# ALiBi and the sliding window as one product with a factor per head, in place of tables on TensorE and biased exponentials on ScalarE

## The chip, the cores and the metric

The kernel runs on one core of a Trainium2 chip. The metric is the device time of one execution in microseconds (us), and every kernel is compared with the kernel before, run in the same rounds on the same chip. The kernel before took 338.57 us (median of 3 runs, 338.24 to 338.61).

## The reference

Sliding-window attention with ALiBi, followed by a feed-forward block (FFN) with a swish. Eight batches, eight heads, 576 positions, 64 numbers a head.

```python
# attention, per batch and head
scores = scale * q @ k.T
rel = pos[:, None] - pos[None, :]
bias = -slopes[h] * abs(rel)                 # slopes 2**-1 ... 2**-8
scores = where((rel >= 0) & (rel < 128), scores + bias, -1e9)
attn = softmax(scores)
x = attn @ v                                 # then 4608 tokens x 512
# FFN
h = x @ w_in                                 # 512 -> 2048
out = (h * sigmoid(beta * h)) @ w_out        # 2048 -> 512
```

The scores are small, so no maximum is subtracted. The weights of a query can be any common multiple, because the sum of the weights divides them.

## The kernel before

One core does all eight batches. TensorE is meant to be busy without a break: the FFN of earlier tokens fills what the attention of the next batch leaves. Batches 0 and 1 come in early, when little else can be done, and are transposed on TensorE in pairs of heads; batches 2 to 7 are transposed by transfers, and their attention is spread between the FFN's matmuls. A "visit" is the scores of two heads for some blocks of keys: 2 x 512 columns (visit B and all visits of batches 2 to 7) or 2 x 384 (visit A).

ALiBi and the window came about in two ways. In batch 0, in the A visits of batch 1 and in both "tail" visits (`SCT`, the last 64 queries of batches 0 and 1), a table with the bias is added on TensorE ahead of the scores, and one exponential follows. In the other visits the bias of the key is the bias pointer of the exponential, so that a visit needs four exponentials, and a product with a mask of zeros and ones follows on VectorE.

```python
def SP_(b, vis, p):                          # a visit of batch 0 or 1
    ...
    for e in range(2):                       # not in the B visits of batch 1
        nc.tensor.matmul(sps[:, e, 0:w], lhsT=ident[:], rhs=table..., start=True, stop=False)
    ...                                      # the scores, added to the table
    nc.scalar.activation(out=pt[:, :, 0:w], in_=sps[:, :, 0:w], func=ACTF.Exp, scale=qscale)

def decayed(pt, sps, p, own, w):
    for e in range(2):
        h = 2 * p + e
        for half, cols in ((0, slice(0, own)), (1, slice(own, w))):
            nc.scalar.activation(out=pt[:, e, cols], in_=sps[e][:, cols], func=ACTF.Exp,
                                 scale=qscale, bias=bias[:, half, h : h + 1])

def SC(b, m, p):                             # a visit of batches 2 to 7
    ...                                      # six matmuls: scores into SS (two banks)
    decayed(pt, sps, p, OWN[m], 512)
    nc.vector.tensor_tensor(out=pt[:], in0=pt[:], in1=masks[m][:], op=ALU.mult)

def TP(b, p):                                # transposes of a pair of heads, k (i=1) then q (i=0)
    for i in (1, 0):
        tps = psum_t.tile([P, FULL], F32, name="tps", tag="t")     # psum_t has 2 slots
        ...                                  # four matmuls with the identity
        (nc.vector.tensor_copy if b or i else nc.scalar.copy)(out=QK[...], in_=tps[:])

def betas():                                 # another user of the same two slots
    bps = psum_t.tile([P, NFF], F32, name="bps", tag="t")
    nc.tensor.transpose(out=bps[:], in_=bflat[:], identity=identf[:])
    nc.vector.tensor_scalar_mul(beta_h[:], bps[:], 0.5)

def Hm(g, j, cs):                            # FFN: four matmuls into a bank hps, then
    ...
    nc.scalar.activation(out=sig[:], in_=hps, func=ACTF.Tanh, scale=beta_h[:, j : j + 1])
    nc.vector.scalar_tensor_tensor(          # gT; it frees the bank
        out=gts[g][:, j, :], in0=sig[:], scalar=1.0, in1=hps, op0=ALU.add, op1=ALU.mult)

# start of the program (cut)
TP(0, 0); SP_(0, "A", 0); SP_(0, "B", 0); tables(2, 4); ones(); cast_pair(0, 1)
TP(0, 1); SP_(0, "A", 1); SP_(0, "B", 1); tables(4, 6); ...; PVP(0, "A", 0); betas(); cast_pair(0, 2)
TP(0, 2); tables(6, 8); ...; SP_(0, "A", 2); SP_(0, "B", 2)
TP(0, 3); PVP(0, "A", 1); SP_(0, "A", 3); SP_(0, "B", 3); ...
```

`PVP` takes weights times values and normalizes on VectorE, `XP` transposes the result for the FFN. The orders of TensorE and of GpSimd (which casts the inputs to bf16) are those of the program throughout. In the start of the program, those of VectorE and ScalarE follow from it too, as compiled.

The softmax here doesn't subtract the row's maximum and nothing guards it: scores larger than these inputs give would overflow.

## Time and profile before

| | before |
|---|---|
| median of 3 runs | 338.57 us |
| span of the profiled execution | 336.8 us |
| busy TensorE / VectorE / ScalarE / GpSimd | 320.8 / 200.0 / 207.0 / 103.5 us |
| mean granted TensorE clock | 1.00 |
| waits of the FFN's banks (hps) for gT | 4.1 us in 8 waits |

The page's busy line and the main groups are in the prediction. This is the view of busy time by stretches of the kernel before; columns: stretch, length, busy us (and instructions) of TensorE's matmuls, its weight loads, VectorE, ScalarE, GpSimd, then granted clock, share of the transfer engines, GB/s.

```profile
8.00:12.00 4.00, 3.50 (x35) 2.17 (x34) 3.70 (x12) 3.30 (x5) 3.64 (x5) 1.00 0.96 289
12.00:16.00 4.00, 3.54 (x35) 2.18 (x33) 2.88 (x7) 2.84 (x5) 3.94 (x7) 1.00 1.22 207
```

TensorE was busy 3.5 us of every 4, at the full clock. This is the start itself, in TensorE's timeline (start, us, engine, line, operation, count, and in brackets the idle time ahead of it with what ended it):

```profile
9.85 0.34 PE L299 MATMUL SS<-qkT 64*128 64x256 bf16 x4 [0.50 <-DVE qkT L252]
...
13.42 0.34 PE L299 MATMUL SS<-qkT 64*128 64x256 bf16 x4 [0.35 <-ACT qkT L252]
...
20.96 0.61 PE L502 MATMUL SX<-XT,W 128*128 128x512 bf16 x2
```

These are the scores of the second and third pair of heads and the first matmul of the FFN.

### The profile page before, as it was taken

Reading aid. Unit: us, or ns where it says so; the run is one execution under the profiler, and the core shown is the slowest. Engines: PE = TensorE matmul, PEld = TensorE weight load, DVE = VectorE, ACT = ScalarE, POOL = GpSimd, SP = SyncE. Lnnn points to the kernel's source line nnn. Section 1 sums busy time; section 2 is a strip of 40 time slices with the busy share of each in tenths; the row PEclk is TensorE's granted clock in tenths of the full one; section 3 lists DMA queues with packets and bytes.
Section 4 is the critical chain, followed back from the end, with each engine's and each line's share of the span. In section 5 each row is a group of like instructions: output and inputs, shape, how many; then the busy total and the mean of one; then the engine's idle time right before and its main releaser. Section 6 shows DMA issues by size and latency. Waiting matters only on the chain.

```text
span 336.8 us, 6208 instructions
## 1 busy us (share of the span) xinstructions
PE 320.8 (95%) x2293; PEld 155.4 (46%) x2293; DVE 200.0 (59%) x435; ACT 207.0 (61%) x405; POOL 103.5 (31%) x177
## 2 busy tenths in 40 slices
PE   8889899999998999999999999999999999999995
PEld 4545454444443454444444444444444444444444
DVE  6757897655468883766187717671778167525500
ACT  3767857565538875778469747774878465345511
POOL 4945630428345337321305142322100100010010
PEclk9999999999999999999999999999999999999999
DMA  7999999999999999991939986997120211210022
GB/s 201 241 283 224 168 201 216 202 197 256 215 224 250 176 217 253 219 201 35 219 80 193 186 200 145 214 161 173 45 58 15 78 47 49 55 64 31 0 85 73
DMA packets 146159, 51.81 MB, mean 154 GB/s; under 512 B 135360, under 2 KB 143824, under 8 KB 146128
## 3 DMA queue, kind: packets, MB, share of 16 engines
q1 hardware_dynamic: 139152, 38.29, 61.4%
q0 software_dynamic: 6944, 13.11, 16.4%
q8 instruction: 18, 0.29, 0.4%
q14 instruction: 13, 0.11, 0.1%
q10 hardware_dynamic: 32, 0.01, 0.0%
HBM read 36.71 MB, written 9.44 MB: 137 GB/s over the span
## 4 chain that ended last, share of the span: by engine, by line
PE 73%; DVE 13%; ACT 10%; issue 3%; DVEq 0%; ACTq 0%
PE ops L528 34%; PE hps L502 26%; ACT pt L319 7%; DVE gT L510 4%; PE SS L418 3%; DVE pt L426 3%; ACT sig L509 2%; PE pv L455 2%; PE hpo L502 2%; DVE qkT L252 1%; PE pv L451 1%; PE SS L103 1%; DVE xnp L337 1%; DVE xn L337 1%; PE SS L299 1%
## 5 line engine op out<-in xcount | busy, mean ns | idle before, releaser
L502 PE MATMUL hps<-XT,W 128*128 128x512 bf16 x540 | 135.2, 379 | 4.5 <-DVE gT L510 4.1
L528 PE MATMUL ops<-W,gT 128*128 128x512 bf16 (+1 forms) x592 | 138.5, 374 | 0.5 <-ACT osb L538 0.5
L510 DVE SCALAR_TENSOR_TENSOR gT<-sig,hps 128x512 bf16<-128x512 bf16 x135 | 91.2, 682 | 65.9 <-ACT sig L509 65.2
L509 ACT ACTIVATE sig<-hps,beta_h 128x512 bf16<-128x512 f32 x135 | 92.5, 695 | 56.3 <-PE hps L502 51.6
L319 ACT ACTIVATE pt<-SS,bias 128x256 bf16<-128x256 f32 (+1 forms) x192 | 75.0, 478 | 15.4 <-PE SS L418 15.4
L528 PEld LDWEIGHTS <-gT 128*128 128x128 bf16 x592 | 54.0, 98 | 57.7 <-issue 2.4
L502 PEld LDWEIGHTS <-W 128*128 128x128 bf16 x576 | 51.7, 98 | 60.5 <-issue 9.5
L545 POOL DMA_DIRECT2D out_dram<-osb x34 | 18.4, 542 | 114.0 <-ACT osb L538 113.8
L426 DVE TENSOR_TENSOR pt<-pt,mask 128x1024 bf16<-128x1024 bf16 x48 | 35.6, 742 | 26.6 <-ACT pt L319 26.5
L538 ACT ACTIVATE osb<-ops 128x512 f32<-128x512 f32 (+1 forms) x28 | 16.6, 592 | 38.3 <-PE ops L528 38.3
L226 POOL CAST vs<-fst 128x512 bf16<-128x512 f32 (+1 forms) x40 | 26.0, 657 | 34.3 <-DMA fst<-in_v_dram 31.2
L211 POOL CAST bst<-fst 128x512 bf16<-128x512 f32 (+1 forms) x32 | 20.7, 646 | 49.0 <-DMA fst<-in_q_dram 35.0
L337 DVE TENSOR_TENSOR xn<-pv,zs 128x256 bf16<-128x256 f32 (+1 forms) x62 | 25.9, 421 | 1.6
L212 POOL CAST bst<-fst 128x512 bf16<-128x512 f32 (+1 forms) x32 | 20.6, 644 | 18.1 <-DMA fst<-in_k_dram 17.9
L455 PE MATMUL pv<-vs,pt 128*128 128x65 bf16 x240 | 21.4, 193 | 0.0
L455 PEld LDWEIGHTS <-pt 128*128 128x128 bf16 x240 | 16.5, 97 | 8.4
L418 PE MATMUL SS<-qkT 64*128 64x256 bf16 (+2 forms) x240 | 18.9, 252 | 1.0 <-ACT pt L319 0.8
L418 PEld LDWEIGHTS <-qkT 64*128 64x128 bf16 x240 | 8.2, 94 | 21.2 <-issue 20.7
L451 PE MATMUL pv<-vs,pt 128*128 128x65 bf16 x192 | 17.9, 193 | 0.0
L451 PEld LDWEIGHTS <-pt 128*128 128x128 bf16 x192 | 15.2, 98 | 5.5
L536 DVE TENSOR_SCALAR osb<-ops 128x512 f32<-128x512 f32 (+1 forms) x9 | 5.9, 657 | 18.6 <-PE ops L528 18.5
L336 DVE RECIPROCAL zs<-pv 128x4 f32<-128x4 f32 (+1 forms) x66 | 11.3, 173 | 9.3 <-PE pv L455 8.2
(83 smaller groups left out, 176.5 us busy)
## 6 DMA issues: line engine op xcount, KB each, us to landing
out_dram<-osb POOLq DMA_DIRECT2D x34, 256.0 KB, 3.1
fst<-in_k_dram SPq DMA_DIRECT2D x32, 256.0 KB, 5.1
fst<-in_q_dram SPq DMA_DIRECT2D x32, 256.0 KB, 4.8
fst<-in_v_dram SPq DMA_DIRECT2D x32, 256.0 KB, 4.4
W<-in_moe_w_in_dram POOLq DMA_DIRECT2D x4, 512.0 KB, 7.3
W<-in_moe_w_out_dram POOLq DMA_DIRECT2D x4, 512.0 KB, 10.7
fst<-in_q_dram SPq DMA_DIRECT2D x8, 128.0 KB, 4.1
fst<-in_k_dram SPq DMA_DIRECT2D x8, 128.0 KB, 4.0
```

Source lines behind the costliest of these rows:

```text
L211: nc.gpsimd.tensor_copy(out=t[0:rows, 0], in_=fs.pop(("q", b, sb))[0:rows])
L226: return nc.gpsimd.tensor_copy(out=VS[b % 2][0:rows, sb, :, 0:D], in_=fs.pop(("v", b, sb))[0:rows])
L319: nc.scalar.activation(out=pt[:, e, cols], in_=sps[e][:, cols], func=ACTF.Exp, scale=qscale, bias=bias[:, half, h : h + 1],)
L337: nc.vector.tensor_tensor(out=xn, in0=pv[0:nq, :, 0:D], in1=zs[0:nq].broadcast_to([nq, 4, D]), op=ALU.mult)
L418: nc.tensor.matmul(o, lhsT=qk[64 * e : 64 * e + 64, 1, p, P * kb : P * kb + P], rhs=qk[64 * e : 64 * e + 64, 0, p, P * kb : P * kb + nq], ...
L426: nc.vector.tensor_tensor(out=pt[:], in0=pt[:], in1=masks[m][:], op=ALU.mult)
L451: nc.tensor.matmul(pv[:, hl, 0 : D + 1], lhsT=weights(b, qb - 1, h, 1), rhs=vs[:, qb - 1, h, 0 : D + 1], start=True, stop=False,)
L455: nc.tensor.matmul(pv[:, hl, 0 : D + 1], lhsT=weights(b, qb, h, 0), rhs=vs[:, qb, h, 0 : D + 1], start=qb == 0, stop=True,)
L502: nc.tensor.matmul(hps, lhsT=W1[:, c, bass.ts(j, P)], rhs=XT[:, c, c0 : c0 + TOKG], start=(c == 0), stop=(c == NDM - 1),)
L509: nc.scalar.activation(out=sig[:], in_=hps, func=ACTF.Tanh, scale=beta_h[:, j : j + 1])
L510: nc.vector.scalar_tensor_tensor(out=gts[g][:, j, :], in0=sig[:], scalar=1.0, in1=hps, op0=ALU.add, op1=ALU.mult)
L528: nc.tensor.matmul(ops_[:, cols], lhsT=gT[:, j, i * P : i * P + P], rhs=W2[:, j, cols], start=(j == 0), stop=(j == NFF - 1),)
```

## The change

The intent: scores are plain in every visit, one exponential covers the whole visit, and ALiBi and the window together are one factor, exp(−slope · distance) inside the window and 0 outside, which takes the mask's place in the product. The tables and their matmuls go. The factors (`fall`, eight heads x 512 columns) are made by ScalarE at the start; two rearranged copies of them (`fallt` for the tails, `fall[1]` for the other kind of visit) are made by VectorE. Since batch 0 and the A visits of batch 1 get a product they did not have, the cast of q in batch 1 goes from VectorE to ScalarE.

```diff
+    def falls(h0, h1):
+        for h in range(h0, h1):
+            nc.scalar.activation(out=fall[0][:, h]..., in_=rel..., func=ACTF.Exp, scale=-slopes[h])
+    def falls_tail():                        # 2 copies of 512 columns on VectorE
+    def falls_late(i):                       # 4 copies, 512 to 1536 columns
-    def biases(): ...   def tables(h0, h1): ...   def constants_masks(): ...   def tail_masks(): ...
@@ TP
-            (nc.vector.tensor_copy if b or i else nc.scalar.copy)(
+            (nc.vector.tensor_copy if i else nc.scalar.copy)(
@@ SP_
-        ... two matmuls of a table with the identity ...
-        if not plain: ... one exponential; return
-        decayed(...)
-        nc.vector.tensor_tensor(... in1=masks[0][:, :, 0:w], op=ALU.mult)
+        nc.scalar.activation(out=pt[:, :, 0:w], in_=sps[:, :, 0:w], func=ACTF.Exp, scale=qscale)
+        nc.vector.tensor_tensor(... in1=fall[0][:, 2 * p : 2 * p + 2, 0:w], op=ALU.mult)
@@ SCT
-        ... two matmuls of a table ...
+        nc.vector.tensor_tensor(out=PC[:, 0:1024], in0=PC[:, 0:1024], in1=fallt..., op=ALU.mult)
@@ SC
-        decayed(pt, sps, p, OWN[m], 512)
-        nc.vector.tensor_tensor(out=pt[:], in0=pt[:], in1=masks[m][:], op=ALU.mult)
+        nc.scalar.activation(out=pt[:], in_=SS[:], func=ACTF.Exp, scale=qscale)
+        nc.vector.tensor_tensor(out=pt[:], in0=pt[:], in1=fall[m][:, 2 * p : 2 * p + 2], op=ALU.mult)
@@ start of the program
-            tables(2, 4) ... tables(4, 6) ... tables(6, 8)
+            falls(5, 6) ... falls(6, 7) ... falls(7, 8)      # falls(0, 5) with the constants
```

More of the change, by code (lines that the diff above doesn't have):

```diff
@@ L48 @@
     qscale = 1.0 / sqrt(D)
-    REF = 63.5
     FAR = 1.0e5
@@ L60 @@
     pen = const.tile([P, P], F32, name="pen")
-    rel = const.tile([P, 3, P], F32, name="rel")
+    rel = const.tile([P, 2, P], F32, name="rel")
     zeros = const.tile([P, 512], BF16, name="zeros")
-    table = const.tile([P, H, 3, P], BF16, name="table")
-    masks = [const.tile([P, 2, 512], BF16, name=f"mask{m}") for m in range(2)]
-    kpos = const.tile([P, 1], F32, name="kpos")
-    bias = const.tile([P, 2, H], F32, name="bias")
+    fall = [const.tile([P, H, 512], BF16, name=f"fall{m}") for m in range(2)]
+    fallt = const.tile([P, 2, 512], BF16, name="fallt")
     PC = const.tile([P, 1024 + 64], BF16, name="pc")
@@ L118, in constants @@
         make_identity(nc, identf[:])
-        nc.gpsimd.iota(
-            kpos[:], pattern=[[0, 1]], base=0, channel_multiplier=1,
-            allow_small_or_imprecise_dtypes=True,
-        )
         for a, cmp in ((0, ALU.is_lt), (1, ALU.is_ge)):
@@ L126, in constants @@
             nc.vector.scalar_tensor_tensor(
-                out=rel[:, 2 * a], in0=qtok[:], scalar=float(P * a), in1=pen[:], op0=ALU.add,
+                out=rel[:, a], in0=qtok[:], scalar=float(P * a), in1=pen[:], op0=ALU.add,
                 op1=ALU.add)
-        nc.vector.tensor_copy(out=rel[:, 1], in_=rel[:, 0])
-        tables(0, 2)
-    def tables(h0, h1):
+        falls(0, 5)
+    def falls(h0, h1):
+        t = rel[:]
         for h in range(h0, h1):
-            nc.vector.tensor_scalar_mul(table[:, h], rel[:], -slopes[h] / qscale)
+            nc.scalar.activation(
+                out=fall[0][:, h].rearrange("k (a n q) -> k a n q", a=2, n=2),
+                in_=bass.AP(tensor=t.tensor, offset=t.offset,
+                            ap=[list(t.ap[0]), [P, 2], [0, 2], [1, P]]),
+                func=ACTF.Exp, scale=-slopes[h])
+    def falls_tail():
+        for at, c in ((0, 0), (256, 256)):
+            nc.vector.tensor_copy(
+                out=fallt[:, :, at : at + 256].rearrange("k e (p q) -> k p e q", q=64),
+                in_=fall[0][:, :, c : c + 64].rearrange("k (p e) q -> k p e q", e=2))
+    def falls_late(i):
+        to, at, w = ((0, 0, 192), (192, 0, P), (320, 256, 64), (384, 256, P))[i]
+        nc.vector.tensor_copy(out=fall[1][:, :, to : to + w], in_=fall[0][:, :, at : at + w])
     def ones():
@@ L144, in padding @@
         nc.gpsimd.memset(PC[:, 1024:], 0.0)
-    def biases():
-        for h in range(H):
-            for half in range(2):
-                nc.vector.tensor_scalar(
-                    out=bias[:, half, h : h + 1], in0=kpos[:], scalar1=-(REF + half * P),
-                    scalar2=slopes[h], op0=ALU.add, op1=ALU.mult,
-                )
     def betas():
@@ L156, in betas @@
         nc.vector.tensor_scalar_mul(beta_h[:], bps[:], 0.5)
-    def fill(m, at, n, w, cmp):
-        t = qtok[:]
-        o = masks[m][:, :, at : at + n * w].rearrange("p e (n w) -> p e n w", w=w)
-        nc.vector.tensor_scalar(
-            out=o, in0=bass.AP(tensor=t.tensor, offset=t.offset,
-                               ap=[list(t.ap[0]), [0, 2], [0, n], [1, w]]),
-            scalar1=0.0, scalar2=None, op0=cmp)
-    def constants_masks():
-        fill(0, 0, 2, P, ALU.is_ge)
-        fill(0, 256, 2, P, ALU.is_lt)
-    def tail_masks():
-        fill(1, 0, 1, P, ALU.is_ge)
-        fill(1, 128, 1, 64, ALU.is_ge)
-        fill(1, 192, 1, P, ALU.is_ge)
-        fill(1, 320, 1, 64, ALU.is_lt)
-        fill(1, 384, 1, P, ALU.is_lt)
     fs = {}
@@ L270 @@
              "B": ((1, 256, 256, P), (2, 0, 256, 256), (3, 128, 384, P))}
-    PLAIN = ((1, "B"),)
     WIDTH = {"A": 384, "B": 512}
@@ L277, in SP_ @@
         w = WIDTH[vis]
-        plain = (b, vis) in PLAIN
-        for e in range(2):
-            if plain:
-                break
-            t = table[:, 2 * p + e]
-            if vis == "A":
-                rhs = t
-            else:
-                rhs = bass.AP(tensor=t.tensor, offset=t.offset,
-                              ap=[list(t.ap[0]), [2 * P, 2], [0, 2], [1, P]])
-            nc.tensor.matmul(
-                sps[:, e, 0:w], lhsT=ident[:], rhs=rhs, start=True, stop=False,
-                skip_group_check=True)
         for kb, at, q0, n in VISIT[vis]:
@@ L301, in SP_ @@
                     rhs=qk[64 * e : 64 * e + 64, 0, p, q0 : q0 + n],
-                    start=plain, stop=True, skip_group_check=True,
+                    start=True, stop=True, skip_group_check=True,
                 )
@@ L305, in SP_ @@
         pts[b, vis, p] = pt
-        if not plain:
-            nc.scalar.activation(
-                out=pt[:, :, 0:w], in_=sps[:, :, 0:w], func=ACTF.Exp, scale=qscale)
-            return
-        decayed(pt, [sps[:, e] for e in range(2)], p, 256, w)
-        nc.vector.tensor_tensor(
-            out=pt[:, :, 0:w], in0=pt[:, :, 0:w], in1=masks[0][:, :, 0:w], op=ALU.mult)
-    def decayed(pt, sps, p, own, w):
-        for e in range(2):
-            h = 2 * p + e
-            for half, cols in ((0, slice(0, own)), (1, slice(own, w))):
-                nc.scalar.activation(
-                    out=pt[:, e, cols], in_=sps[e][:, cols], func=ACTF.Exp,
-                    scale=qscale, bias=bias[:, half, h : h + 1],
-                )
+        nc.scalar.activation(out=pt[:, :, 0:w], in_=sps[:, :, 0:w], func=ACTF.Exp, scale=qscale)
+        nc.vector.tensor_tensor(
+            out=pt[:, :, 0:w], in0=pt[:, :, 0:w], in1=fall[0][:, 2 * p : 2 * p + 2, 0:w],
+            op=ALU.mult)
     def room(b, shape, i):
@@ L368, in SCT @@
         qk = QK[b % 2]
-        for e in range(2):
-            t = table[:, e]
-            rhs = bass.AP(tensor=t.tensor, offset=t.offset,
-                          ap=[list(t.ap[0]), [2 * P, 2], [6 * P, NP], [1, 64]])
-            nc.tensor.matmul(
-                SS[:, e, :], lhsT=ident[:], rhs=rhs, start=True, stop=False, skip_group_check=True)
         for p in range(NP):
@@ L381, in SCT @@
                         rhs=qk[64 * e : 64 * e + 64, 0, p, FULL:S],
-                        start=False, stop=True, skip_group_check=True,
+                        start=True, stop=True, skip_group_check=True,
                     )
@@ L386, in SCT @@
             scale=qscale)
+        nc.vector.tensor_tensor(
+            out=PC[:, 0:1024], in0=PC[:, 0:1024], in1=fallt[:].rearrange("k e w -> k (e w)"),
+            op=ALU.mult)
     def DT(b, sb):
@@ L401 @@
     COLS = {0: (0, 384), 1: (128, 256), 2: (0, 384), 3: (192, 320), 4: (128, None)}
-    OWN = (256, 320)
     def SC(b, m, p):
@@ L406, in SC @@
         qk = QK[b % 2]
-        sps = [SS[:, e] for e in range(2)]
         for kb in ((0, 1), (2, 4, 3))[m]:
@@ L411, in SC @@
             for e in range(2):
-                o = sps[e][:, at : at + min(nq, 512 - at)]
+                o = SS[:, e, at : at + min(nq, 512 - at)]
                 if kb in (0, 2):
@@ L424, in SC @@
         pt = pt_pool.tile([P, 2, 512], BF16, name="pt", tag="pt")
-        decayed(pt, sps, p, OWN[m], 512)
-        nc.vector.tensor_tensor(out=pt[:], in0=pt[:], in1=masks[m][:], op=ALU.mult)
+        nc.scalar.activation(out=pt[:], in_=SS[:], func=ACTF.Exp, scale=qscale)
+        nc.vector.tensor_tensor(
+            out=pt[:], in0=pt[:], in1=fall[m][:, 2 * p : 2 * p + 2], op=ALU.mult)
         pts[b, m, p] = pt
@@ L624 @@
             SP_(0, "B", 0)
-            tables(2, 4)
+            falls(5, 6)
             ones()
@@ L630 @@
             SP_(0, "B", 1)
-            tables(4, 6)
+            falls(6, 7)
             cast_v(0, 0)
@@ L637 @@
             TP(0, 2)
-            tables(6, 8)
+            falls(7, 8)
             w1.append(load_w1(0))
@@ L752, in open_o @@
                 tc.tile_pool(name="psum_o", bufs=2, space=bass.MemoryType.PSUM))
-        steps = [h[2], biases, constants_masks, h[3], R(0), h[4], A(0), h[5], B_(0), R(1), h[6],
+        steps = [h[2], h[3], R(0), h[4], A(0), h[5], B_(0), R(1), h[6],
                  A(1), B_(1), R(2), h[7], A(2), R(3), B_(2), A(3), h[8], B_(3), open_o, VA(0),
-                 h[9], VA(1), h[10], VA(2), tail_masks, lambda: TT(0), h[11], VA(3),
+                 h[9], VA(1), h[10], VA(2), falls_tail, lambda: TT(0), h[11], VA(3),
                  lambda: SCT(0), VB(0), h[12], VB(1), lambda: PV(0, 4, 0), VB(2), h[13], XO(0),
@@ L769 @@
         items += o[6:]
-        spread([wrap(it) for it in items], 22, len(items) - 2, need[2])
+        for n in range(4):
+            items.insert(12 + n, lambda n=n: falls_late(n))
+        spread([wrap(it) for it in items], 26, len(items) - 2, need[2])
         for g in range(2, NTG):
```

## The prediction

> **What bounds the kernel now.** I read the page first, then the chain that ended last, the waits, and the timelines of four places: the head (0 to 26 us), the visits of batch 1 (25 to 50 us), one crowded stretch of batch 2, and some later stalls. The page:
>
> ```profile
> PE 320.8 (95%) x2293; PEld 155.4 (46%) x2293; DVE 200.0 (59%) x435; ACT 207.0 (61%) x405; POOL 103.5 (31%) x177
> L502 PE MATMUL hps<-XT,W 128*128 128x512 bf16 x540 | 135.2, 379 | 4.5 <-DVE gT L510 4.1
> L319 ACT ACTIVATE pt<-SS,bias 128x256 bf16<-128x256 f32 (+1 forms) x192 | 75.0, 478 | 15.4 <-PE SS L418 15.4
> L426 DVE TENSOR_TENSOR pt<-pt,mask 128x1024 bf16<-128x1024 bf16 x48 | 35.6, 742 | 26.6 <-ACT pt L319 26.5
> ```
>
> TensorE is the bound over the whole; ScalarE has 39% free, so the 75 us of exponentials are not on the path as a sum. What they cost is read in TensorE's waits. Whole wait lists of PE: hps for gT 4.1 us (8 times, longest 0.84), SS for the cast of qkT 1.5 + 0.9, SS for an exponential 0.8, pvo for an exponential 0.8, the rest below 1. The matmuls themselves cannot wait less than they stream; in the chain that ended last stands
>
> ```profile
> 291.41 6.91 PE ops L528 x32
> ```
>
> which is 0.216 us for 512 columns. One stall after the head, from the timeline of all engines (ScalarE, VectorE and TensorE rows):
>
> ```profile
> 166.87 1.56 ACT L319 ACTIVATE pt<-SS,bias 128x256 bf16<-128x256 f32 x4
> ...
> 168.29 0.71 ACT L509 ACTIVATE sig<-hps,beta_h 128x512 bf16<-128x512 f32 x1
> 168.46 1.21 DVE L426 TENSOR_TENSOR pt<-pt,mask 128x1024 bf16<-128x1024 bf16 x1 [0.77 <-ACT pt L319]
> ...
> 169.59 0.68 DVE L510 SCALAR_TENSOR_TENSOR gT<-sig,hps 128x512 bf16<-128x512 bf16 x1
> ...
> 170.32 1.02 PE L502 MATMUL hps<-XT,W 128*128 128x512 bf16 x4 [0.57 <-DVE gT L510]
> ```
>
> The reader is to see a queue: four exponentials hold ScalarE 1.56 us, the tanh stands behind them, the mask product stands before gT on VectorE, and TensorE waits 0.57 us for a bank of hps. The other gT waits that I looked at have the same shape. The head is different: it is a chain of small dependent steps.
>
> ```profile
> 16.28 0.34 PE L299 MATMUL SS<-qkT 64*128 64x256 bf16 x4 [0.17 <-ACT qkT L252]
> ...
> 17.53 1.02 ACT L307 ACTIVATE pt<-SX 128x1024 bf16<-128x1024 f32 x1
> ...
> 17.82 0.18 DVE L336 RECIPROCAL zs<-pvh 128x4 f32<-128x4 f32 x1 [1.35 <-PE pvh L352]
> ```
>
> The scores of the fourth pair start at 16.28, and six normalizations of batch 0 start on VectorE at 17.82, while ScalarE is still in the last exponential; they end at 21.43. VectorE has nothing to do for batch 0's weights there. That is what the change takes away.
>
> **What the Trainium skill says.** "ScalarE: Activation LUTs", section "What ACT_TABLE_LOAD costs": an activation with immediate scale and bias takes 186 ns + 0.833 ns a column, each per-partition pointer 93 ns more, and neighbours overlap by about 93 ns. The trace agrees: 1.024 us for 1024 columns, 0.817 for 768, 0.479 for 256 with the bias pointer, four of them 1.56. "VectorE: DVE Perf Modes", section "What auto-detection actually checks": tensor_tensor reaches two elements a cycle at most. Agreed: 674 to 692 ns for an undisturbed mask product of 1024 columns. I estimate 0.57 for 768 from it (128 cycles of 0.96 GHz fewer). "SBUF — State Buffer", section "Who interferes with whom": a VectorE instruction with two SBUF inputs contends with a GpSimd instruction that reads SBUF, and the second to issue blocks. The product at 40.97 agrees: 1.19 us, beside a GpSimd cast that began at 40.59. "PSUM — Partial Sum Buffer", section "Engine vs sequencer instructions": VectorE and ScalarE are strict FIFO. So the compiled order of VectorE decides the head, and I read it for the changed kernel.
>
> **The change, part by part.**
>
> Steady state (batches 2 to 7, 48 visits). Four exponentials (1.56) become one of 1024 columns (1.02): 0.54 us less on ScalarE each, 26 us in all, and the score banks come free 0.54 sooner. The product stays (same 1024 columns, another operand). TensorE does nothing less. The worth is therefore what its stalls lose, at most 0.54 each. The gT waits of 0.84, 0.32, 0.56, 0.57, 0.27, 0.58, 0.67 and some 0.29 lose 0.54 + 0.32 + 0.54 + 0.54 + 0.27 + 0.54 + 0.54 + 0.29 = 3.6; the wait of the scores for an exponential, 0.8, loses 0.5. Together −4.1 us.
>
> Tables on TensorE. Gone are 16 matmuls of 384 columns (0.162 us each), 8 of 512 and 4 of 512 (0.216): 5.2 us of streaming. Most lie where TensorE then waits for qkT anyway: in the head all of them are hidden by the chain below. The two of the second tail visit, in the FFN stretch around 70 us where TensorE is 100% busy, are real: −0.4.
>
> Batch 1. Per pair ScalarE loses 1.56 − 1.02 and gains one cast of q (0.585), VectorE loses that cast (0.69) and gains the product of visit A (0.57). Sums are even, but the two casts of a pair now run side by side instead of 1.28 us in a row. Walking the new order from the first transposes of batch 1 (25.64 before): scores of pairs 0 to 3 start 1.75, 5.6, 8.6 and 10.6 us later, against 2.6, 6.6, 9.25 and 11.8 in the trace; the last exponential ends some 1.3 us earlier, which frees the bank that pvo waits for. −1.2. Against it, the tail visit of batch 0 has a product of 0.69 between its exponential (ends 46.08) and weights that TensorE takes at 46.32: +0.5.
>
> Head. Every pair has now exponential A, exponential B, product A, product B, and only then, in VectorE's compiled order, the next pair's cast of k. Starting from unchanged scores of pair 0 at 6.84 (the first five factors fit: 2.7 to 5.4 on ScalarE, before its cast at 6.20):
> - exponential B of pair 0 ends 9.1; product 0.7 to 1.0 (GpSimd casts beside it); cast of k 0.65; scores of pair 1 at 10.6 to 10.9 (trace: 9.85).
> - their exponentials to 12.8–13.1, product to 13.6–14.1, the normalization and beta that stand before the cast to 14.3–14.9, cast of k; scores of pair 2 at 15.1–15.6 (13.42).
> - exponential A to 16.3–16.8, B to 17.3–17.9; the copies of the factors for the tails were put here by the scheduler, mostly into idle time, some 0.3 late; product B to 18.1–19.3, cast; scores of pair 3 at 18.8–20.1 (16.28).
> - its exponentials to 21.0–22.3, last product to 21.8–23.1, and only after it the six normalizations (3.6 us as before): end at 25.3–26.6 (21.43).
>
> So 3.9 to 5.2 us later; I take +4.3, as the first tables and masks on VectorE (4.5 and 2.0 us busy) leave it.
>
> Sum: 338.57 − 4.1 − 0.4 − 1.2 + 0.5 + 4.3 = 337.7. Large pieces that cancel.
>
> **Rivals.**
> 1. The head costs little: the copies, products and casts overlap better than my walk, +1 to +2[...]. For it: in the trace some VectorE rows of the head are contended by GpSimd already, so that the walk double counts. Time: 333 to 335.
> 2. VectorE takes the place of ScalarE: between 97 and 113 us it is busy 12.15 of 16 us against ScalarE's 13.04, and the product there is not smaller. The gT waits then shrink by half only, −2, and the head stays: about 340. Against it: in every stall read, the product was itself waiting for the fourth exponential.
> 3. ScalarE's 26 us were the price of the whole, as the groups suggest: then 312. TensorE at 95% refuses it: stalls in all the rows of PE are some 13 us, and the first microseconds are not touched.
> 4. The new factors collide with GpSimd's casts and weights' descriptors until 50 us, and W lands later: 343 and more. W waits are not in PE's list at all, so unlikely.
>
> **Range and chances.** The head is uncertain by about 2 us, the steady part by 1.5, batch 1 by 1, the order of instructions by 1.5: together about 3. Eight in ten: 333.0 to 342.0. Faster by over 2% needs below 331.8, which takes the best of every part: 0.08. Slower by over 2% needs above 345.3: 0.05. Within 2%: 0.87.
>
> **What would show it.** The head is right if the first hps matmul of W (20.96 before) starts near 25, with VectorE's products before the six normalizations; wrong if before 22.5. Batch 1 is right if the stretch from its first transposes to its last exponential is about 14 us (15.3 before). The steady part is right if the wait of hps for gT drops from 4.1 to about 0.5 in sum and the stretch from 113 us to the end is shorter by 3 to 4 us; a new wait of hps for a gT that stands behind products alone would mean rival 2. The prediction as a whole is wrong if ScalarE's busy time falls by about 26 us and the head is not longer.

## The result

The changed kernel took 341.33 us (median of 4 runs, 341.26 to 342.52) against 338.59 (338.24 to 339.2) of the kernel before in the same rounds, with correct output. The ratio is 1.0087, with a 95% interval of 1.0061 to 1.0114. Ratios here are from the fast runs of both kernels in the same rounds, so not quite the ratio of the medians quoted. Executions over 1.5% slower than the fastest of the same kernel are left out of the means. The verdict is "same" at 2%, but the changed kernel is surely a little slower. The span of its profiled execution was 339.5 us against 336.8, at a mean granted clock of 0.98 against 1.00.

The lines of the changed kernel's page that answer to those in the prediction, with its row of clocks:

```profile
PE 318.2 (94%) x2265; PEld 156.1 (46%) x2265; DVE 207.3 (61%) x419; ACT 186.3 (55%) x261; POOL 106.8 (31%) x176
...
PEclk9777999999999999999999999999999999999999
...
L453 PE MATMUL hps<-XT,W 128*128 128x512 bf16 x540 | 135.4, 380 | 2.6 <-DVE gT L461 2.2
...
L375 ACT ACTIVATE pt<-SS 128x1024 bf16<-128x1024 f32 x48 | 48.9, 1019 | 22.0 <-PE SS L368 22.0
...
L376 DVE TENSOR_TENSOR pt<-pt,fall 128x1024 bf16<-128x1024 bf16 x48 | 40.8, 850 | 24.4 <-ACT pt L375 24.2
```

ScalarE did what was asked: 75.0 us of exponentials in batches 2 to 7 became 48.9, and its whole busy time fell by 20.7 us. The waits for gT fell from 4.1 to 2.2 us. Two things are new. The same 48 products cost 850 ns on average instead of 742. And in the row of clocks, slices 1 to 3 (8.5 to 34 us) show about seven tenths, where the kernel before had nine in every slice.

**Where the time went.** Both traces have the same 2265 matmuls in the same order once the 28 table matmuls are left out. So I paired them and read the lag: the start in the changed kernel minus the start in the kernel before.

| stretch (time of the kernel before) | lag at its end | change over it |
|---|---|---|
| start to 10.7 us | 0.0 | 0.0 |
| to 26.4 us (batch 0; first transposes of batch 1) | 6.9 | +6.9 |
| to 45 us (batch 1) | 5.1 | −1.8 |
| to 48 us (tail visit of batch 0) | 5.8 | +0.7 |
| to 67 us (tail visit of batch 1) | 5.3 | −0.5, of it −0.4 at the visit |
| to 90 us (start of batch 2) | 6.2 | +0.85 |
| to the end | 2.6 | −3.5 |

The sum, +2.6, is the difference of the spans within 0.1. The later parts behave, and the head takes more than they give.

**The head.** TensorE's timeline of the changed kernel:

```profile
10.53 0.34 PE L267 MATMUL SS<-qkT 64*128 64x256 bf16 x4 [2.13 <-DVE qkT L234]
...
14.33 1.01 PE L232 MATMUL tps<-ident,bst 128*128 128x128 bf16 x4 [2.26 <-DVE beta_h L158]
...
16.02 0.51 PE L267 MATMUL SS<-qkT 64*128 64x256 bf16 x4 [0.67 <-ACT qkT L234]
...
16.88 1.89 PE L232 MATMUL tps<-ident,bst 128*128 128x128 bf16 x8
...
20.60 0.34 PE L267 MATMUL SS<-qkT 64*128 64x256 bf16 x4 [1.50 <-DVE qkT L234]
...
27.16 1.49 PE L453 MATMUL SX<-XT,W 128*128 128x512 bf16 x3
```

The scores of pairs 1, 2 and 3 start at 10.53, 16.02 and 20.60, and the first FFN matmul at 27.16 instead of 20.96. Two entries were not in my walk. The transposes of q at 14.33 waited 2.26 us, not for data, but for a slot: `beta_h` on VectorE had to empty one of the two slots that the transposes use. And the durations are odd: eight transposes take 1.89 us, where the kernel before has eight in 1.05, and three FFN matmuls take 1.49. VectorE in the same stretch:

```profile
11.75 1.90 DVE L275 TENSOR_TENSOR pt<-pt,fall 128x768 bf16<-128x768 bf16 x2 [1.28 <-ACT pt L274]
...
14.11 0.17 DVE L158 TENSOR_SCALAR beta_h<-bps 128x16 f32<-128x16 f32 x1
14.19 0.68 DVE L234 CAST qkT<-tps 128x512 bf16<-128x512 f32 x1
16.53 0.90 DVE L137 COPY fallt<-fall 128x512 bf16<-128x512 bf16 x2 [1.65 <-ACT fall L129]
17.35 0.96 DVE L143 COPY fall<-fall 128x1536 bf16<-128x1536 bf16 x1
18.23 0.54 DVE L275 TENSOR_TENSOR pt<-pt,fall 128x768 bf16<-128x768 bf16 x1
18.69 0.65 DVE L143 COPY fall<-fall 128x1024 bf16<-128x1024 bf16 x2
19.27 0.68 DVE L275 TENSOR_TENSOR pt<-pt,fall 128x1024 bf16<-128x1024 bf16 x1
19.87 0.68 DVE L234 CAST qkT<-tps 128x512 bf16<-128x512 f32 x1
```

VectorE takes its instructions in the compiled order: the cast at 19.87 reads transposes that had ended at 18.77, and still came after what stands ahead of it. `beta_h` stands behind two products and a normalization. The cast of k that releases the scores at 20.60 stands behind two products and the copies of the factors. The busy time by stretches shows the other new thing (columns as before):

```profile
8.00:12.00 4.00, 1.87 (x25) 1.25 (x24) 2.35 (x6) 2.95 (x5) 3.20 (x5) 1.00 1.10 308
12.00:16.00 4.00, 1.09 (x5) 0.63 (x4) 2.81 (x6) 1.77 (x4) 4.00 (x6) 0.55 1.19 186
```

Where TensorE had been busy 3.5 us of 4, it is now busy 1.87 and then 1.09, and the granted clock is 0.55. These are means over stretches. The record itself knows two values here: half from 12.4 to 19.2 and from 22.6 to 29.4 us, and full between them and after. Half clock doubles the time of the transposes and of the first FFN matmuls (the eight at 16.88 follow one another at 0.213 us, and at 0.109 us with the clock at 1.00 in e2): three of 512 columns in 1.49 us are some 0.43 us each beside the lead of the first, where the kernel before has 0.216.

**The steady part.** Of the stall like the one in the prediction, with only the rows of VectorE and GpSimd and the matmul that waits:

```profile
172.58 1.75 DVE L376 TENSOR_TENSOR pt<-pt,fall 128x1024 bf16<-128x1024 bf16 x1 [0.23 <-ACT pt L375]
172.61 0.61 POOL L193 CAST bst<-fst 128x512 bf16<-128x512 f32 x1
...
173.17 0.60 POOL L194 CAST bst<-fst 128x512 bf16<-128x512 f32 x1
...
174.25 0.67 DVE L461 SCALAR_TENSOR_TENSOR gT<-sig,hps 128x512 bf16<-128x512 bf16 x1
...
174.98 0.81 PE L453 MATMUL hps<-XT,W 128*128 128x512 bf16 x3 [0.57 <-DVE gT L461]
```

The four exponentials are gone, and TensorE still waits 0.57 us, as it did in the prediction's stall. The product, two inputs from SBUF, takes 1.75 us instead of 0.69 beside GpSimd's casts and ends 0.55 us after the last of them (173.77), and gT comes behind it. In all, 11 of the 48 products take more than 760 ns (8 in the kernel before), and each of them ends 0.54 to 0.56 us after the end of a cast, in both kernels. The largest is new in its size; the kernel before has none over 1.21:

```profile
86.86 2.96 DVE L376 TENSOR_TENSOR pt<-pt,fall 128x1024 bf16<-128x1024 bf16 x1 [0.69 <-ACT pt L375]
```

Four casts run from 87.00 to 89.27, and the product ends 0.55 us after them. Behind it the lag grows by 0.6 (TensorE waits for a bank of the output that VectorE empties late); the other 0.2 of the 0.85 come earlier, at 75.8 us of the kernel before.

### The profile page after: what moved, and what is told of

It reads as the page before. It is cut to its first block, busy times and chain, and to the rows that moved or that the text cites. A ratio compares the mean times of both kernels' runs of the same rounds, so it can differ in the third digit from the quotient of the medians.

```text
span 339.5 us, 5989 instructions
## 1 busy us (share of the span) xinstructions
PE 318.2 (94%) x2265; PEld 156.1 (46%) x2265; DVE 207.3 (61%) x419; ACT 186.3 (55%) x261; POOL 106.8 (31%) x176
## 3 DMA queue, kind: packets, MB, share of 16 engines
q0 software_dynamic: 6944, 13.11, 15.1%
## 4 chain that ended last, share of the span: by engine, by line
PE 70%; DVE 12%; ACT 7%; issue 4%; DMA 4%; SPq 2%; POOL 1%; POOLq 0%; ACTq 0%; DVEq 0%
PE ops L479 30%; PE hps L453 26%; PE SS L368 3%; DVE pt L376 3%; DVE gT L461 3%; ACT pt L375 3%; DMA fst<-in_q_dram 2%; ACT pt L274 2%; DVE pt L275 2%; PE tps L232 2%; PE pv L406 1%; PE hpo L453 1%; ACT sig L460 1%; PE pv L402 1%; DMA qkT<-bst 1%
## 5 line engine op out<-in xcount | busy, mean ns | idle before, releaser
L461 DVE SCALAR_TENSOR_TENSOR gT<-sig,hps 128x512 bf16<-128x512 bf16 x135 | 92.2, 684 | 66.7 <-ACT sig L460 65.4
L375 ACT ACTIVATE pt<-SS 128x1024 bf16<-128x1024 f32 x48 | 48.9, 1019 | 22.0 <-PE SS L368 22.0
L376 DVE TENSOR_TENSOR pt<-pt,fall 128x1024 bf16<-128x1024 bf16 x48 | 40.8, 850 | 24.4 <-ACT pt L375 24.2
L208 POOL CAST vs<-fst 128x512 bf16<-128x512 f32 (+1 forms) x40 | 27.5, 694 | 31.3 <-DMA fst<-in_v_dram 27.5
L193 POOL CAST bst<-fst 128x512 bf16<-128x512 f32 (+1 forms) x32 | 21.1, 660 | 41.2 <-DMA fst<-in_q_dram 35.3
L194 POOL CAST bst<-fst 128x512 bf16<-128x512 f32 (+1 forms) x32 | 21.0, 657 | 14.0 <-DMA fst<-in_k_dram 14.0
L275 DVE TENSOR_TENSOR pt<-pt,fall 128x768 bf16<-128x768 bf16 (+1 forms) x16 | 11.2, 711 | 4.2 <-ACT pt L274 4.1
```

What stands on the lines that cost most here:

```text
L193: nc.gpsimd.tensor_copy(out=t[0:rows, 0], in_=fs.pop(("q", b, sb))[0:rows])
L208: return nc.gpsimd.tensor_copy(out=VS[b % 2][0:rows, sb, :, 0:D], in_=fs.pop(("v", b, sb))[0:rows])
L375: nc.scalar.activation(out=pt[:], in_=SS[:], func=ACTF.Exp, scale=qscale)
L376: nc.vector.tensor_tensor(out=pt[:], in0=pt[:], in1=fall[m][:, 2 * p : 2 * p + 2], op=ALU.mult)
L461: nc.vector.scalar_tensor_tensor(out=gts[g][:, j, :], in0=sig[:], scalar=1.0, in1=hps, op0=ALU.add, op1=ALU.mult)
```

## The experiments

The theories: the head's 6.9 us come from (1) the slot that `beta_h` holds, (2) the fallen clock, (3) the order of products and casts on VectorE, (4) the copies of the factors ahead of them; the steady part gains about 4 us by itself, and GpSimd's reads take back a part of it. Below, "changed" is the changed kernel and all lags are of profiled runs. The runs of one kernel spread by 1 us and more, and three kernels had a run 2.5 us and more above their median. e1 to e4, e5 to e8, and e9 with the repetition ran on three chips, each group beside the kernel before.

### e1_beta_first: the scaling of beta ahead of everything

```diff
+            betas()
             cast_pair(0, 0)
             TP(0, 0)
@@
             PVP(0, "A", 0)
-            betas()
             cast_pair(0, 2)
```

> The changed kernel, with the transpose and copy of beta moved ahead of batch 0's first pair, so that its PSUM slot is free early. Theory A (the slot that beta holds stops TensorE for 2.3 us in the transposes of pair 2): that wait vanishes, the scores of pair 2 start near 14.9 instead of 16.02, and the time falls by 1.0 to 1.5 us from the changed kernel's 341.3, to about 340.1. Rival (the chain of products on VectorE sets the pace alone): the wait moves to the cast of k, and the time falls by under 0.5 us.

Measured: 342.33 us (341.17 to 344.0), ratio 1.0114 [1.0083, 1.0145]. The wait is gone, and the scores of pair 2 start at 14.90 as expected. But VectorE then does this:

```profile
14.76 1.51 DVE L137 COPY fallt<-fall 128x512 bf16<-128x512 bf16 x2
16.20 2.31 DVE L143 COPY fall<-fall 128x1536 bf16<-128x1536 bf16 x3
18.43 0.54 DVE L275 TENSOR_TENSOR pt<-pt,fall 128x768 bf16<-128x768 bf16 x1
```

The copies come earlier too and last 3.7 us in a row, the product stands behind them until 18.43, and the scores of pair 3 start at 20.60, to the hundredth as without the edit. What follows: the slot was a real wait of 2.3 us, and alone it was worth nothing, because the copies were hidden behind it. The clock was at half for as long as without the edit (13.7 us).

### e2_fillers: matmuls of zeros where TensorE waits

```diff
-    def TP(b, p):
+    def TP(b, p, fill=0):
+            if not i:
+                idle(fill)                    # matmuls of zeros between the k and the q half
@@
             TP(0, 1)
+            idle(8)
@@
-            TP(0, 2)
+            TP(0, 2, 9)
@@
+            idle(6)
             SP_(0, "A", 3)
@@
             PVP(0, "B", 0)
+            idle(7)
```

> The changed kernel, with 30 idle matmuls of zeros into the score bank in TensorE's four long waits of the head. Theory B (the waits let the granted TensorE clock fall to about half from some 14 to 30 us, and that costs time of its own): the granted clock of the head stays at 1.00, matmuls of 128 columns follow at about 55 ns instead of 213 ns or 107 ns, and the time falls by 1 to 2 us to about 339.8. Rival (the slow clock lies in waits only): the clock is restored but the time stays at 341.3 within 0.4.

Measured: 340.31 us (339.56 to 341.41), ratio 1.0049 [1.0025, 1.0074], against 1.0085 to 1.0114 of the other two variants of the changed kernel in these rounds. The granted clock is 1.00 in every stretch of the head, and the lag against the changed kernel is −1.8 us from 32 us on (−1.5 to −2.1 on the way, −1.8 at the end). The profiled run is the fastest of its six. TensorE:

```profile
15.86 1.05 PE L234 MATMUL tps<-ident,bst 128*128 128x128 bf16 x8
...
26.08 0.66 PE L455 MATMUL SX<-XT,W 128*128 128x512 bf16 x2
```

The eight transposes take 1.05 us again, and two FFN matmuls 0.66. What follows: the fallen clock costs some 1 to 2 us of the head (1.8 in the profile, 1.0 to 2.0 between medians), and it comes from TensorE having little to do. The tables, which looked like hidden waste, had been a part of what kept it busy: between 8 and 16 us TensorE was busy 7.0 us in the kernel before, 5.2 without the table matmuls, and 3.0 in the changed kernel. So the longer waits took more of its work away than the missing tables did.

### e3_casts_first: products of batch 0 after the next pair's cast

```diff
+        if b:
+            MU(b, vis, p)                     # batch 1 as it was
+    def MU(b, vis, p):                        # the product with the factor, by itself
+        ...
@@
             TP(0, 1)
+            MU(0, "A", 0)
             SP_(0, "A", 1)
             SP_(0, "B", 1)
+            MU(0, "B", 0)
@@
-            PVP(0, "A", 0)
@@
             TP(0, 2)
+            PVP(0, "A", 0)
+            MU(0, "A", 1)
...                                            # and so on; the last ones between the normalizations
```

> The changed kernel, with VectorE's order in batch 0 changed: the cast of k of the next pair before the products of the pair before, the last products between the normalizations. Theory C (products queued ahead of the casts and the normalizations make the head longer): the first matmul of W moves from 27.2 to about 23 us, and the time falls by 4 to 5 us, to 336.5 to 337.5. Rival (factors on ScalarE and the copies of factors make it): the first matmul of W stays after 25.5 and the time falls by 1 to 2.

Measured: 342.16 us (339.91 to 342.36), ratio 1.0085 [1.0057, 1.0114]. The profiled run was its fastest, with a lag of −0.9 to −1.4 us against the changed kernel from 32 us on. The scores of pairs 1, 2 and 3 start at 10.31, 13.95 and 18.54: earlier by 0.2, 2.1 and 2.1, but pair 3 is far from the 16.28 of the kernel before, and the first FFN matmul starts at 26.59, where the theory had 23 and the rival "after 25.5". VectorE shows why:

```profile
16.93 0.95 DVE L143 COPY fall<-fall 128x1536 bf16<-128x1536 bf16 x1
17.81 0.67 DVE L234 CAST qkT<-tps 128x512 bf16<-128x512 f32 x1
```

The copies took the place of the products ahead of the cast of k. The expectation fell short: order is one of the causes, and alone it is worth little (nothing between the medians, 1.4 us in its fastest run).

### e4_steady_only: the kernel before, with batches 2 to 7 alone changed

```diff
@@ SC, in the kernel before
-        decayed(pt, sps, p, OWN[m], 512)
-        nc.vector.tensor_tensor(out=pt[:], in0=pt[:], in1=masks[m][:], op=ALU.mult)
+        nc.scalar.activation(out=pt[:], in_=SS[:], func=ACTF.Exp, scale=qscale)
+        nc.vector.tensor_tensor(
+            out=pt[:], in0=pt[:], in1=fall[m][:, 2 * p : 2 * p + 2], op=ALU.mult)
@@ the factors and their copies, spread over the FFN of the second token group
+            after(r, last[-1])                # each waits for an FFN matmul issued shortly before
+        for n in range(4):
+            items.insert(9 + 2 * n, lambda n=n: falls_late(n))
+        for n in range(8):
+            items.insert(1 + 2 * n, lambda n=n: falls(n, n + 1))
```

> The kernel before, with only the 48 visits of batches 2 to 7 changed to one exponential and a product with factors that are built on ScalarE between 50 and 65 us; tables, batch 1 and the tails as before. Theory D (the visits of batches 2 to 7 win by themselves what the trace shows after 97 us, 3.4 us): 338.6 - 3 = about 335.6, the head as before. Rival (the 3.4 us is only the long head's delay caught up again, as transfers are no longer waited for): 338.0 to 338.6.

Measured: 335.83 us (335.27 to 336.54), ratio 0.9915 [0.9895, 0.9936], output correct, clock 1.00. Against the kernel before the lag is +0.2 in the head and +1.2 at 92 us (the factors cost something where they are made, and a product of 2.41 us stands at 82.5), then it goes to −3.3 at the end: −4.5 from 92 us on, −3.9 from 67 us on. Its waits:

```profile
PE hps L521 <- DVE gT L530: 1.4, 3, 0.6
```

What follows: the steady part is worth what was predicted of it, and this kernel beats both.

### e5_copies_late: the copies of the factors after the head

```diff
+    last = []                                 # Hm appends its last matmul
@@ falls_tail, falls_late
-            nc.vector.tensor_copy(
+            r = nc.vector.tensor_copy(...)
+            after(r, last[-1])
```

> The changed kernel, with only this changed: the six copies that build the factors of the tails wait for a matmul of the FFN, so that the scheduler can't put them into the head. Theory F (they stand on VectorE before the products and the cast of k of pairs 2 and 3, 0.9 us or more of path): the scores of pair 3 start at 19.8 or before instead of 20.60, the first matmul of W near 26.2, the time 1 us less than the changed kernel's 341.3. Rival (they only fill idle time, as the prediction had it, 0.3): 341.0 or more.

Measured: 341.74 us (339.35 to 342.38, and one run of 345.48, left out of the ratio), ratio 1.0061 [1.0026, 1.0095]. The scores of pair 3 start at 20.04 (19.8 or before expected). The lag against the changed kernel is −0.8 at 24 us, −1.0 at 32 us and −0.3 at the end; some was lost again between 45 and 60 us, around the tail visit of batch 0. The sign is as expected, but the gain at the end is within the spread: inconclusive by itself.

### e6_q_on_dve: the cast of q in batch 1 back on VectorE

```diff
-            (nc.vector.tensor_copy if i else nc.scalar.copy)(
+            (nc.vector.tensor_copy if b or i else nc.scalar.copy)(
```

> The changed kernel, with the casts of q of batch 1 back on VectorE, as in the kernel before. Theory G (the two casts of a pair side by side are what makes the stretch of batch 1 shorter by 1.8 us): from the first transposes of batch 1 to the end of its visits it takes 1 to 1.8 us longer, 342.3 to 343.1. Rival (the single exponential of 1.02 for 1.56 us makes it): within 0.5 of 341.3.

Measured: 348.56 us (346.98 to 350.15), ratio 1.0271 [1.0235, 1.0307]. The direction was right and the size more than three times larger. Against the changed kernel, the lag goes from +0.3 to +6.2 us within batch 1 (32 to 45 us):

```profile
PE SS L267 <- DVE qkT L234: 8.6, 6, 2.1
```

Two of these six waits are those of the head, which the changed kernel has too (3.6 us in 2). The four of batch 1 are 5.0 us, the longest 1.6, and behind them the granted clock was at half once more, from 46.7 to 53.6 us: a cast on an engine that also has products and gT in its queue costs far more than its own 0.69 us. So the move of this cast to ScalarE is what makes the change bearable in batch 1.

### e7_all_three: e1, e3 and e5 together

```diff
+            betas()                           # first, as in e1
+            MU(0, "A", 0)  ...                # products after casts, as in e3
+            after(r, last[-1])                # copies late, as in e5
```

> The changed kernel with three repairs of the head together: beta ahead of the first pair, the casts of k ahead of the products with the last products between the normalizations, the copies of factors out of the head. Theory (these three waits are the head): the scores of pair 3 start near 16 to 16.5, the first matmul of W near 22.5 instead of 27.2, the granted clock stays at 1.0, time 341.3 - 4.7 = about 336.6 or less. Rival (16 products and the factors on ScalarE keep the head long however they are ordered): first matmul of W after 25, time above 339.

Measured: 337.81 us (336.31 to 340.89), ratio 0.9967 [0.9925, 1.0009], so not told apart from the kernel before. The scores of pair 3 start at 16.21 as expected and the first FFN matmul near 22.7 us; the time is 1.2 us above the expected 336.6. The lag against the changed kernel is −4.9 at 24 us, −4.5 at 28 us and −4.7 at the end. By themselves the three gave about 0, −1.4 and −0.3 at the end. What follows: together they are worth far more than the sum of single repairs. That each repair alone uncovers the next wait is what e1 and e3 show. But a part of the gain is the clock: it was at half for 3.4 us here (19.9 to 23.3), for 13.7 us in the changed kernel, and e2 puts that at 1 to 2 us. Waits and clock are not told apart by this run.

### e8_few_reads: GpSimd reads a quarter (wrong result)

```diff
@@ cast_qk, cast_v: from batch 2 on, only 2 of 8 heads are cast, the rest is set to zero
+        n = 2 if b >= 2 else H
+        if n < H:
+            nc.gpsimd.memset(t[0:rows, :, n:], 0.0)
-        nc.gpsimd.tensor_copy(out=t[0:rows, 0], in_=fs.pop(("q", b, sb))[0:rows])
+        nc.gpsimd.tensor_copy(out=t[0:rows, 0, 0:n], in_=fs.pop(("q", b, sb))[0:rows, 0:n])
```

> The changed kernel, wrong on purpose: GpSimd casts only two of eight heads of q, k and v of batches 2 to 7 and fills the others with zeros, so that it works about as long but reads a quarter of the data. Theory H (what is left of the waits of hps for gT, 2.2 us, and the stalls of 0.85 us between 76 and 92, come from products held up by GpSimd's reads): the mean product falls from 850 ns to under 720, the waits of hps for gT to under 0.7, the time by 1.5 to 3 us. Rival (VectorE's queue itself is full): product unchanged or waits unchanged, 341 or more.

Measured: 338.44 us (337.18 to 340.69), ratio 0.9983 [0.9948, 1.0017]; the output is wrong as intended (relative error 0.49). Over the steady part it gains 1.8 us on the changed kernel (lag −0.6 at 60 us, −2.4 at the end), although a new wait of 1.4 us for a transfer stands in its list (hps for XT). Of the waits for gT one of 0.3 us is left, and the products (minimum, median and maximum in ns) are

```profile
L382 DVE TENSOR_TENSOR pt<-pt,fall x48: 681/693/811, 77.3 to 279.4; 128x1024 bf16<-128x1024 bf16 x48
```

where the changed kernel's longest was 2964. What follows: the remaining gT waits come from GpSimd's reads beside the products, not from products that are too many. GpSimd was busy as long (108.3 us against 106.8), with zeroing in place of most of its reading, and 14 products that overlap the zeroing take 691 to 694 ns. So it is the reading that counts.

### e9_tables_batch0: the changed kernel with batch 0 back on tables

```diff
@@ SP_
+            if b:
+                break                         # tables for batch 0 alone, as before
...
-                    start=True, stop=True, skip_group_check=True,
+                    start=b > 0, stop=True, skip_group_check=True,
+        if b == 0:
+            return                            # no product
@@ start: tables(2, 4), (4, 6), (6, 8) back; falls(5, 8) after XP(0, 2); copies as in e5
```

> The changed kernel, with batch 0 alone back on tables (added by TensorE, no product), the factors built on ScalarE before and after batch 0's visits, the copies for the tails kept out of the head. Theory (the change loses 6.9 us in batch 0 alone, and gains 1.8 in batch 1 and 3.4 or more after 97 us): the first matmul of W back near 21 to 22 us, the granted clock 1.00, time 333 to 334.5, 1.2 to 1.6% below the kernel before. Rival (the gains in the later stretches are the head's delay caught up): 337 or more.

Measured: 336.17 us (335.33 to 339.16), ratio 0.9931 [0.9897, 0.9966]: faster than the kernel before, not as fast as expected, and not better than e4. The profiled run was one of the two slowest of its six (338.2). In it the lag against the kernel before is −1.6 us at 69 us and +2.4 at 75, first because of one wait for a transfer that brings batch 2:

```profile
PE SS L393 <- DMA qkT<-bst: 2.3, 1, 2.3
```

The wait explains 2.5 of these 4.1 us. The other 1.6 are the clock again: right behind the wait it was at half from 73.1 to 76.5 us. What follows: without the head's loss, batch 1's gain is real, but the kernel then reaches batch 2 before batch 2's data. The trace shows this in one of the slower runs. Three of the six runs list a mean clock of 0.994 or 0.995, among them the two slowest (3.4 us at half take 0.005 off the mean), the others 0.999 or 1.00; whether all runs have the wait is open.

### after_again: the changed kernel once more, on another chip

No edit.

> The changed kernel unaltered, beside the kernel before on the same chip as the run above: 341.3, ratio 1.009, granted clock 0.975 to 0.98; first matmul of W at 27.2 within 0.5. Were the ratio under 1.003, the differences of the experiments of about 1 us would be chip to chip.

Measured: 341.96 us (341.11 to 344.24), ratio 1.0104 [1.0075, 1.0133], clock 0.97. The result repeats, with the first FFN matmul near 28.05, further off than the 0.5 expected around 27.2. Its lag at the end is 1.0 us above that of the first profile. Differences of one profiled run below 1 us are not to be read on their own.

## Why the prediction was right or wrong

The class, within 2%, was right, and 341.33 lies inside the range, near its upper end. The sum was 3.6 us too low, and its sign was wrong: 0.9 us faster was forecast, 2.7 slower came. That 341.33 still lies inside is due to the width of the range, 9 us, and not to the terms. Term by term:

| term | predicted | measured (lag) |
|---|---|---|
| head | +4.3 | +6.9 |
| batch 1 | −1.2 | −1.8 |
| tail visit of batch 0 | +0.5 | +0.7 |
| tables of the second tail visit | −0.4 | −0.4 |
| steady part, batches 2 to 7 (67 us to the end) | −4.1 | −2.7 |
| of it the start of batch 2 (67 to 90 us) | none | +0.85 |
| of it 90 us to the end | | −3.5 |

**Head: mechanism right, size wrong.** The chain of products before casts and normalizations is there: pair 1 came at 10.53 (10.6 to 10.9 predicted), the six normalizations start behind the last product at 23.35 and end at 27.6 (25.3 to 26.6 predicted). The step that failed is the walk from pair 2 on. Pair 2 was to start at 15.1 to 15.6 and started at 16.02, pair 3 at 18.8 to 20.1 and started at 20.60. Three things were missing in it. First, "the normalization and beta that stand before the cast" were counted as VectorE's time (`beta_h` itself takes 0.17 us), but beta also holds one of two slots, and the transposes of q waited 2.3 us for it. I followed data and not buffers. Second, the copies of the factors "mostly into idle time, some 0.3 late": in the trace they stand between products and casts, and one of 1536 columns took 0.96 us beside GpSimd's casts. Third, the clock: I took each TensorE duration from the kernel before and left the tables out as "hidden by the chain". They were hidden, but without them and with the longer waits TensorE was busy 27% of a stretch, its clock fell to half, and the filler run puts this at 1 to 2 us. e1, e3, e5 and e7 show that the waits for the slot, the order and the copies do not add up from single repairs: about 0, −1.4 and −0.3 at the end alone, −4.7 together, a part of it the clock.

**Batch 1 and the tail visits: right.** The stretch from the first transposes to the first product of weights and values of batch 1, which waits for the last exponential, went from 15.35 us to 13.36 (about 14 predicted). e6 shows what carries it: with the cast of q on VectorE it is 6 us longer. One reading is off: the product at 40.97, cited for the collision, ends 0.95 us after the cast named, not 0.54 to 0.56 like the held products of batches 2 to 7, so that cast alone does not explain it.

**Steady part: right in kind, its parts off.** gT's waits were to fall to about 0.5 and fell to 2.2; the step that failed is the worth of each gT wait as the excess of four exponentials over one, 3.6 in sum. They lost 1.9. Three waits of 0.56, 0.57 and 0.58 us (at 148, 170 and 216 us in the kernel before) came through whole: 0.57, 0.57 and 0.58. The product ahead of each took 1.07, 1.21 and 1.07 us before, and 1.61, 1.75 and 1.61 after. Against TensorE's matmuls it starts 0.54 us earlier, is held 0.54 us longer, and in both kernels ends 0.55 us after a cast of GpSimd. So the four exponentials were not what these waits stood for. The prediction's own lines had the sign: the product at 168.46 takes 1.21 us, where an undisturbed one takes 0.69.

With fewer reads (e8) most of what was left of the gT waits is gone (2.2 to 0.3). Over batches 2 to 7 the lag falls by 2.7, not 4.1, and from 113 us on by 2.4, where the prediction's sign was 3 to 4. e4 reaches −3.9 from 67 us on, and still has two waits of 0.58 behind products of 1.76 and 1.61 us; so the loss depends on which product meets which cast. The waits of gT are not the whole of it, and I did not trace every other part.

**Rivals.** Rival 2, VectorE in ScalarE's place with waits that shrink by half and about 340 us, came closest, but for another reason: not VectorE's load (busy 207.3 of 339.5 us) but its collision with GpSimd. Rival 1, a cheap head, is refuted by the first FFN matmul at 27.16. Rival 3 is refuted by TensorE's 94%. Rival 4 named GpSimd's casts but put the cost into late weights; no wait for W shows.

**Start of batch 2: missed.** Of the 0.85 us, 0.6 come behind the one product of 2.96 us. Each of e1, e2, e3, e5 and the repetition has this product too, and loses 0.85 us between 72 and 89 us. e7 has no such product there and loses 0.2; so does e8, which takes the reads away on purpose.

**What stays open.** How much of e3's and e5's small gains is spread; how much of e7's gain is the clock; whether the wait for batch 2's transfer is in all runs of e9; and what exactly makes the clock fall, of which the runs show only that filling the gaps prevents it.

## What to carry to other kernels

Work that is hidden behind a wait need not be free to remove at a kernel's start: look at how busy TensorE stays without it, and at the granted clock by stretches. When an engine takes over work in a chain of small steps, walk its compiled queue for buffers as well as for data, and do not be surprised when single repairs show little until the waits behind them are gone too. Before counting a wait as won, check how long the steps of its chain take undisturbed: a product that ends at a fixed time after another engine's cast gains nothing from starting earlier. The part of a change that pays can be taken alone: the steady visits by themselves gave 335.83 us, where the whole change gave 341.33.

## What the Trainium skill lacked or had wrong

- "TensorE: Matmul & The Clock Gate", section "HAM oscillation — how this bites in real kernels", puts the rule as "no PE-idle gaps >~3.4µs". Here the longest gaps between 8 and 16 us were 2.13 and 2.26 us, with 1.5 us of matmuls between them, and the granted clock was 0.55 from 12 to 16 us. So gaps that are each shorter than that can be enough when little stands between them; with filler matmuls in them the clock was 1.00. In e9 a single gap of 2.32 us (69.75 to 72.07), with TensorE busy 3.75 of the 3.80 us before it, was followed by half clock from 73.1 to 76.5 us. The two speeds that the page gives, in section "Wait — 56ns, not 53.3ns?", agree: 0.216 and some 0.43 us for 512 columns.
- "SBUF — State Buffer", section "Who interferes with whom", says that a VectorE instruction with two SBUF inputs contends with a GpSimd instruction that reads SBUF, which e8 confirms (longest product 811 ns with a quarter of the reads, 2964 with all). It says that whoever issues first has the ports for its whole instruction. It does not say what happens when such reads follow one another: where the next cast began before the last had ended, the product was held through the whole row (2.96 us at 86.86, through four casts). All 11 held products ended 0.54 to 0.56 us after the end of a cast. The start in the profile does not tell who is held: that product started 0.14 us before the first of the four casts.
